# Wait lists, weight loads in pieces and a new operation order in a two-layer recurrent-memory transformer kernel

## The chip, the cores and the metric

The kernel runs on one core of one Trainium2 chip. The metric is the device time of one execution in microseconds (us). Each kernel was executed several times, and the medians are quoted. A ratio is the mean time of one kernel's fast runs over that of the kernel before in the same rounds, so it is not quite the ratio of the medians that stand beside it. Engines: PE is TensorE, PEld its weight loads, DVE VectorE, ACT ScalarE, POOL GpSimd, SP the engine that issues most transfers. In the profile's lines L128, L131 or L138 is one helper that issues all matmuls; its line number differs from kernel to kernel.

## The reference

A segment-recurrent attention layer (A) and a gated feed-forward layer (B), both applied twice with the same weights. In A, each of 64 segments of 32 tokens attends to itself and to 8 memory tokens, and the output rows of the memory are the memory of the next segment. That makes the chain which everything else has to fit around.

```python
def _A_ref(x, mem0, Wq, Wk, Wv, Wo, seg_len):          # cut
    mem = mem0
    for s in range(n_seg):
        h = jnp.concatenate([mem, x[:, s*seg_len:(s+1)*seg_len, :]], axis=1)
        q, k, v = (jnp.einsum('btd,dhe->bhte', h, W) for W in (Wq, Wk, Wv))
        scores = jnp.where(mask, jnp.einsum('bhqe,bhke->bhqk', q, k) * scale, -1e9)
        o = jnp.einsum('bhqk,bhke->bhqe', _softmax(scores), v)
        o = jnp.einsum('bhte,hed->btd', o, Wo)
        mem = o[:, :M, :]
        outs.append(o[:, M:, :])
def _B_ref(x, W_gate, W_up, W_down):                    # cut
    return (relu(x @ W_gate) * (x @ W_up)) @ W_down
x = x + _A_ref(_layernorm(x), ...);  x = x + _B_ref(_layernorm(x), ...)
x = x + _A_ref(_layernorm(x), ...);  x = x + _B_ref(_layernorm(x), ...)
```

## The kernel before

The kernel first multiplies the weights together (Wq with Wk, Wv with Wo), then runs 68 steps in which the first application of A works on one segment and the second on the segment four behind. Four steps repeat as one **period**. In a step the memory's chain is: s_mem (scores, softmax on DVE and ACT), p_t (transpose), u_mem, un_mem (the new memory in PSUM), hi (ACT) and lo (DVE: memory minus hi), then selm on PE (it moves hi and lo to where the next step needs them). All other work (t_block, u_seg, un, the glu of layer B: names of groups of matmuls in the code) is filler beside that chain.

Python lists all operations, a small scheduler puts them in an order from two tables (SLOT, BIAS), and then semaphores are laid. What matters here is how an operation gets its waits:

```python
def _need(self, eng, reads, writes):
    need = {}                       # semaphore -> value, one per engine or transfer
    ...                             # writers of what is read, readers of what is overwritten
    out = []
    for src, val in need.items():
        if self.known[eng].get(src, 0) < val:       # this engine hasn't waited for it yet
            self.known[eng][src] = val
            out.append((self.sems[src].sem, val))
    return out
...
    for s, v in waits:
        E.wait_ge(s, v)
    fn(E).then_inc(ev.sem, 1)
```

In the built program one wait of this list, the first, stays on the instruction itself (**attached**); the others go to instructions of their own ahead of it, with one or two waits each (**stand-alone**; counts of stand-alone waits below are counts of these instructions). And how the feed-forward weights are loaded, as soon as the buffers that they reuse are free:

```python
for h, W, d, n in ((0, S.Wg, S.Wg_d, "Wg"), (1, S.Wu, S.Wu_d, "Wu")):
    S.q.add("dma", ..., E.dma_start(W, d[0:384, :]...), (), where[n] + [(n,)])              # 1344 KB
    S.q.add("dma", ..., E.dma_start(S.W3[64*h:64*h+64, :], d[384:448, :]), ...)             # 224 KB
S.q.add("dma", ..., E.dma_start(S.Wd, S.Wd_d...), (), where["Wd"] + [("Wd",)])              # 1568 KB
```

## Time and profile before

| | kernel before |
|---|---|
| median | 1586.51 us (1584.45 to 1588.66, 4 runs) |
| profiled span | 1582.5 us |
| pure stream of PE | 1461.6 us |
| lost by PE up to its last matmul's start | 116.9 us |
| mean period (13 periods) | 89.82 us |
| half clock | six stretches, 27.1 us together |

**Pure stream** and **lost time** are used all through this document. The stream is every matmul of the built program times the distance at which matmuls of its form follow one another in the records when nothing holds them, plus 96 ns per change of the array's tile shape. The start of a matmul in the records, less the stream up to it, is what PE has lost so far: by standing, by waiting or by half clock. It is an estimate worked out from records.

One more view, the list of waits of PE from 200 to 1480 us (whom it waited for: us in total, number of times, longest):

```profile
PE b L128 <- DVE lo L1061: 7.9, 11, 1.5
PE b L128 <- ACT TTs L773: 5.1, 10, 0.5
PE b L128 <- issue: 4.5, 10, 0.8
PE b L128 <- DMA PTs<-Ps: 3.2, 5, 0.8
PE b L128 <- DVE Em L958: 2.8, 12, 0.2
```

The names to the right of the arrow are what PE waited for: lo; TTs, the copy by which ACT empties a bank of PSUM for t_block; PTs, the transposed probabilities of the segment, which a transfer brings; Em, a step of the memory's softmax; "issue" is time with no wait that the profile shows. Read it as a ranking, not as a sum: a pipelined matmul row hides short gaps, so this list sees less than the start-to-start count. The longest item is lo, the end of the memory's chain.

### The profile page before, as it was taken

Reading aid. Unit: us, or ns where it says so; the run is one execution under the profiler, and the core shown is the slowest. Engines: PE = TensorE matmul, PEld = TensorE weight load, DVE = VectorE, ACT = ScalarE, POOL = GpSimd, SP = SyncE. Lnnn points to the kernel's source line nnn. Section 1 sums busy time; section 2 is a strip of 40 time slices with the busy share of each in tenths; the row PEclk is TensorE's granted clock in tenths of the full one; section 3 lists DMA queues with packets and bytes.
Section 4 is the critical chain, followed back from the end, with each engine's and each line's share of the span. In section 5 each row is a group of like instructions: output and inputs, shape, how many; then the busy total and the mean of one; then the engine's idle time right before and its main releaser. Section 6 shows DMA issues by size and latency. Waiting matters only on the chain. (4 is left out here: it accounts for less than half of the span.)

```text
span 1582.5 us, 82606 instructions
## 1 busy us (share of the span) xinstructions
PE 1509.5 (95%) x37849; PEld 1110.3 (70%) x37849; DVE 877.3 (55%) x2316; ACT 865.7 (55%) x2636; POOL 111.3 (7%) x259
## 2 busy tenths in 40 slices
PE   5979999999999999999999999999999999999998
PEld 2556666777676776777676777777677777767675
DVE  7434556555555656554554655555564655555554
ACT  5734554655555565655556565555556465554432
POOL 4000000000000000000000000000000000000000
PEclk9989999999999999999999999999999999999999
DMA  9920000101000101001000101000010001000000
GB/s 211 239 71 12 19 18 19 20 15 17 19 16 15 25 15 19 16 16 19 16 19 15 21 18 15 17 19 16 18 21 15 20 19 15 15 18 15 18 19 14
DMA packets 128715, 46.05 MB, mean 29 GB/s; under 512 B 117480, under 2 KB 127472, under 8 KB 128368
## 3 DMA queue, kind: packets, MB, share of 16 engines
q1 hardware_dynamic: 128016, 40.52, 12.5%
q8 instruction: 298, 4.88, 1.3%
q14 instruction: 49, 0.40, 0.1%
q10 hardware_dynamic: 352, 0.24, 0.1%
HBM read 10.33 MB, written 1.84 MB: 8 GB/s over the span
## 5 line engine op out<-in xcount | busy, mean ns | idle before, releaser
L128 PE MATMUL b<-hT,Mw 128*128 128x80 bf16 (+1 forms) x11424 | 442.0, 200 | 6.4 <-issue 5.2
L128 PEld LDWEIGHTS b<-hT,Mw 128*128 128x128 bf16 x11424 | 418.7, 100 | 24.7 <-issue 13.0
L773 ACT ACTIVATE TTs<-b 128x320 bf16<-128x320 f32 (+4 forms) x694 | 290.0, 420 | 5.4 <-PE b L128 4.2
L128 PE MATMUL b<-Nw,big 128*32 128x448 bf16 (+1 forms) x3504 | 291.2, 353 | 0.3 <-issue 0.3
L773 ACT ACTIVATE TTm<-b 128x80 bf16<-128x80 f32 (+5 forms) x696 | 161.6, 232 | 218.9 <-PE b L128 211.1
L128 PEld LDWEIGHTS b<-Nw,big 128*32 128x32 bf16 (+1 forms) x3504 | 139.7, 97 | 99.4 <-issue 3.2
L128 PE MATMUL b<-xBT,big 128*128 128x128 bf16 (+3 forms) x4900 | 206.8, 215 | 1.9 <-issue 1.1
L128 PEld LDWEIGHTS b<-xBT,big 128*128 128x128 bf16 (+1 forms) x4900 | 186.3, 102 | 17.0 <-issue 7.5
L128 PE MATMUL b<-Nw,UTm 128*32 128x448 bf16 x3752 | 191.7, 356 | 1.8 <-ACT UTm L773 1.3
L128 PE MATMUL b<-hT,M 64*64 64x80 bf16 (+2 forms) x7208 | 149.2, 199 | 13.8 <-ACT TTs L773 5.1
L128 PEld LDWEIGHTS b<-Nw,UTm 128*32 128x32 bf16 x3752 | 100.4, 97 | 82.3 <-issue 11.3
L128 PEld LDWEIGHTS b<-hT,M 64*64 64x64 bf16 (+1 forms) x7208 | 113.3, 108 | 46.5 <-issue 24.5
L773 ACT ACTIVATE big<-b 128x512 bf16<-128x512 f32 (+1 forms) x244 | 123.5, 551 | 38.8 <-PE b L128 37.5
L774 POOL COPY hK<-xn 32x448 bf16<-32x448 bf16 x136 | 75.0, 552 | 662.1 <-DVE xn L816 655.7
L774 DVE CAST TTm<-b 64x64 bf16<-64x64 f32 (+5 forms) x188 | 41.3, 219 | 142.0 <-PE b L128 140.1
L774 DVE CAST big<-b 128x512 bf16<-128x512 f32 x144 | 82.3, 597 | 67.0 <-PE b L128 66.8
L1227 ACT ACTIVATE gT<-b 128x512 bf16<-128x512 f32 (+2 forms) x128 | 69.4, 542 | 64.2 <-PE b L128 63.5
L773 ACT ACTIVATE UTm<-b 128x512 bf16<-128x512 f32 (+1 forms) x143 | 81.7, 574 | 38.2 <-PE b L128 38.2
L128 PE MATMUL b<-big,hB 128*128 128x448 bf16 (+1 forms) x574 | 99.8, 354 | 0.3 <-DVE hB L1228 0.3
L1228 DVE TENSOR_TENSOR hB<-gT,b 128x512 bf16<-128x512 bf16 (+2 forms) x128 | 77.8, 619 | 27.5 <-ACT gT L1227 14.8
L128 PE MATMUL b<-PTs,hK 40*64 40x512 bf16 (+1 forms) x1024 | 83.3, 364 | 9.7 <-DMA PTs<-Ps 5.6
L957 DVE TENSOR_REDUCE stat<-b 128x2 f32<-128x80 f32 (+1 forms) x67 | 15.9, 237 | 136.1 <-PE b L128 135.0
(112 smaller groups left out, 1600.1 us busy)
## 6 DMA issues: line engine op xcount, KB each, us to landing
big<-in_A_Wo_dram SPq DMA_DIRECT2D x3, 896.0 KB, 5.8
out_dram<-ys SPq DMA_DIRECT2D x32, 56.0 KB, 1.9
big<-in_B_W_down_dram SPq DMA_DIRECT2D x1, 1568.0 KB, 8.5
XA<-in_A_x_dram SPq DMA_DIRECT2D x28, 56.0 KB, 2.6
big<-in_B_W_up_dram SPq DMA_DIRECT2D x1, 1344.0 KB, 8.5
big<-in_B_W_gate_dram SPq DMA_DIRECT2D x1, 1344.0 KB, 11.5
PTs<-Ps SPq DMA_TRANSPOSE x67, 2.5
Nw<-in_A_Wo_dram SPq DMA_DIRECT2D x1, 896.0 KB, 6.5
```

Of the source, the lines that this page charges most:

```text
L128: ins = E.matmul(out, lhsT=lhsT, rhs=rhs, **kw)
L773: return E.activation(out(), src(), ACT.Copy)
L774: return E.tensor_copy(out(), src())
L957: S.dve(lambda E: E.tensor_reduce(st[:, 32:32 + nl], src(), AX.X, ALU.max), n, C.res(), [("sm", 0)])
L1227: S.act(lambda E, g=g, R=R, n=n: E.activation(S.gT[:, g, 0:n], R[0].b()[:, 0:n], ACT.Relu), n, R[0].res(), [("gT", g)])
L1228: S.dve(lambda E, g=g, R=R, n=n, fcs=fcs: E.tensor_tensor(S.hB[:, fcs[0]:fcs[-1] + 1, 0:w], S.gT[:, g, 0:n].rearrange("p (a b) -> p a b", ...
```

## The change

Its intent: fewer and better placed waits; weight loads that don't stand in front of the small transposes which the chain needs; and a new search of the order with a cost model that knows that an ACT or DVE instruction whose start partitions change is held until the one before has ended. The core of the diff (the tables of some 170 searched numbers, BIAS and SLOT, are replaced as a whole):

```diff
+        need = {src: val for src, val in need.items() if kn.get(src, 0) < val}
+        past = {src: self.seen[src, val] for src, val in need.items()}
         out = []
+        for src, val in sorted(need.items(), key=lambda x: -self.when[x]):
+            if not any(p.get(src, 0) >= val for other, p in past.items() if other != src):
+                out.append((self.sems[src].sem, val))
         for src, val in need.items():
-            if kn.get(src, 0) < val:
-                kn[src] = val
-                out.append((self.sems[src].sem, val))
+            for a, v in [(src, val)] + list(past[src].items()):
+                if kn.get(a, 0) < v:
+                    kn[a] = v
 ...
-        return 35.0 if b != "pe" else 140.0 if a == "act" else 95.0
+        return 60.0 if b == "pe" else 35.0
 ...
+        fit = {"act": 104.0, "dve": 84.0}
+        def start(e, o):
+            if e not in fit:
+                return free[e]
+            return max(0.0, free[e] + (-fit[e] if o.base == base[e] else 28.0))
 ...
+        def piece(n, i, out, src):
+            S.pieces.append(lambda key: S.q.add("dma", ..., E.dma_start(out, src), [key], where[n] + [(n, i)]))
+        for n, W, d, m in (("Wu", ..., range(4)), ("W3", ..., range(2)), ("Wg", ..., range(6)), ("Wu", ..., range(4, 6))):
+            ...                                    # 224 KB each
+        for i in range(7):
+            piece("Wd", i, S.Wd[:, 2 * i:2 * i + 2, :], ...)
 ...
     def mm(self, fn, cost, rd, wr, mode=0, alt=None):
+        due = bool(self.pieces) and q.cat in self.PACE.get(q.t, ())     # steps 0 and 1 only
+        key = [("pace", len(self.pieces))] if due else []
-        self.q.add("pe", ("pe",), {"pe": cost}, fn, rd, wr, mode=mode, alt=alt)
+        q.add("pe", ("pe",), {"pe": cost}, fn, rd, list(wr) + key, mode=mode, alt=alt)
+        if due:
+            self.pieces.pop(0)(key[0])             # this piece may go when that PE operation is done
```

`when` is the time at which the scheduler's model has an event end; `seen` is what the engine that set it had itself waited for, so that a wait implied by another one is recognised.

## The prediction

> **What bounds the kernel now.** I read the page first (busy shares and slices), then the sums by window, then the timeline around single gaps, and last the trace's records of starts and semaphore increments. The page:
>
> ```profile
> PE 1509.5 (95%) x37849; PEld 1110.3 (70%) x37849; DVE 877.3 (55%) x2316; ACT 865.7 (55%) x2636; POOL 111.3 (7%) x259
> ...
> PE   5979999999999999999999999999999999999998
> ...
> PEclk9989999999999999999999999999999999999999
> DMA  9920000101000101001000101000010001000000
> ```
>
> TensorE (PE) is nearly full from the third slice on (each slice is 40 us), both copy engines stand at 55%, and the DMA engines matter in the first two or three slices only. So the end is set by PE: the time of its stream plus its gaps. Four steps of the recurrence repeat as one period. Two of them in the sums by window (busy us and instruction counts, then granted clock, DMA share, GB/s):
>
> ```profile
> 245.67:335.86 90.19, 88.07 (x2223) 65.88 (x2219) 50.26 (x127) 50.80 (x154) 5.79 (x14) 1.00 0.09 18
> 335.86:426.11 90.25, 88.03 (x2222) 65.87 (x2219) 50.27 (x127) 51.09 (x154) 5.79 (x14) 1.00 0.10 18
> ```
>
> Only 2.15 us of 90.2 shows as idle, but a busy matmul row is pipelined. I therefore took the start-to-start distance of neighbouring matmuls from the records (36 ns for 128x80, 189.5 for 128x448, 56 for 128x128, and so on) and called everything above that, plus 96 ns where the tile shape of the array changes, a gap. This gives 3.02 us of gaps per period, 45 us in 200 to 1480 us, and 97 us in the whole run, the slow-clock stretches of the start included. The largest kind in the period, from the timeline (start, length, engine, line, operation):
>
> ```profile
> 783.60 1.69 PE L128 MATMUL b<-Nw,big 128*32 128x448 bf16 x32
> 783.82 0.54 ACT L1060 ACTIVATE hi<-b 128x448 bf16<-128x448 f32 x1 [1.64 <-PE b L128]
> 784.47 0.63 DVE L1061 TENSOR_TENSOR lo<-b,hi 128x448 bf16<-128x448 f32 x1 [1.00 <-ACT hi L1060]
> ...
> 785.21 0.13 PEld L128 LDWEIGHTS b<-selm,hi 128*32 128x32 bf16 x4 [0.37 <-issue]
> ```
>
> The new memory leaves PE as hi and lo, and the next PE operation (selm) needs both. PE does 32 other matmuls meanwhile, then stands. The records show that lo's semaphore came 135 ns before selm's first matmul.
>
> The start has another cause:
>
> ```profile
> 73.76 0.37 SPq L731 DMA_DIRECT2D big<-in_B_W_down_dram  x1
> 74.22 0.65 SPq L727 DMA_DIRECT2D big<-in_B_W_gate_dram  x1
> 76.23 2.04 SPq L866 DMA_TRANSPOSE PTs<-Ps  x1
> ...
> 86.36 0.64 PE L128 MATMUL b<-PTs,hK 40*64 40x512 bf16 x2 [2.40 <-DMA PTs<-Ps]
> ```
>
> The small transpose PTs was issued at 76.2 and landed at 86.1 us, against 2.5 us in the page's list of issues: 2.9 MB of down and gate weights were in front of it (12 us at the 241 GB/s of slice two). PE stood 2.4 us, and its clock was halved:
>
> ```profile
> 82.90:93.10 10.20, 7.65 (x197) 6.32 (x193) 4.22 (x18) 2.93 (x11) 0.00 (x0) 0.50 0.43 79
> ```
>
> **What the Trainium skill says.** (1) Perfetto Trace Analysis, Identifying Dependency Chains: an instruction that waits for several engines may get EventSemaphore instructions ahead of it. The trace agrees: 606 on PE (51 ns each), 369 on DVE (21 ns), 116 on ACT (17 ns). In the built program the first wait in the list stays on the instruction and the others become such instructions. (2) TensorE: Matmul & The Clock Gate, Part 1: after an idle window of some 3.4 us the array runs at half rate. The trace agrees: seven pieces at 0.5, of 3.4 or 10.2 us. (3) TensorEngine Tiling (Array Packing), Key Properties: a change of tiling mode drains the array. Here the step from a 128x80 full matmul to a 64x64 tile takes 132 ns and not 36. (4) VectorE: DVE Perf Modes, Two Vector instructions with no wait between them: an instruction whose start quadrant differs from the one before is held. The trace agrees, for ACT too: with no wait between, the next starts 104 ns before the end of the one before if quadrants agree (ACT), 24 ns after it if not; on DVE 84 before, 31 after.
>
> **Part 1, the waits.** Where the last event to arrive sits on the instruction, PE's first matmul follows 43 ns later; where it sits on a stand-alone wait, 135 ns later. The same pair is 23 and 93 ns on DVE, 23 and 83 on ACT. So "latest first" is worth 92 ns where PE really waits. The trace has 143 such boundaries, 8 a period; 143 x 92 = 13 us at most, if every one of them stayed. Standalone waits fall from 605 to 367 on PE, from 369 to 108 on DVE and from 198 to 11 on SP; one that was satisfied long ago costs PE nothing (with one ahead, 128x40 matmuls still follow at 25 ns), so that count itself is worth about 0.
>
> **Part 2, the new order.** Counting matmuls of the built programs with the same distances, PE's pure stream is 1461.6 us before and 1463.9 after: 774 tile changes become 796, all of the added ones in the first and last steps, and the repeated period is equal at 86.2 us. So nothing is gained in the stream; gains are in gaps alone. I counted, in the built order, how much PE work lies between a producer and its consumer in one period, and held it against the latency that the trace shows:
> - un_mem to selm (hi, lo): 1824 ns before. Of it 92 (PE) and 70 (DVE, lo waits for hi by a stand-alone wait) go: 1662. Work between: 1695, 2074, 1624, 1036 ns before; 1695, 4727, 1624, 3420 after. Gap 0.89 us a period before, 0.04 after. **This is the main gain: 0.85 x 14.2 periods = 12 us.**
> - u_mem to un_mem: 925 ns with the wait attached; least work between 976 before, 597 after: 0.07 becomes 0.33.
> - s_mem: least work 686 before, 415 after, against some 510: adds 0.1.
> - t_block and u_seg, which wait until ACT has emptied a bank: 0.78 + 0.37 before. 3 x 92 ns go. Quadrant changes fall from 560 to 425 on ACT and 562 to 518 on DVE, so ACT's queue is 135 x 128 ns = 17 us shorter, and some of its lateness should go. I take 0.65 after.
> - PTs late (0.27), gaps inside runs of matmuls with no wait at all, which I take for instruction fetch (0.47), small ones (0.17): unchanged.
> After: 0.04 + 0.33 + 0.1 + 0.65 + 0.27 + 0.47 + 0.17 = 2.03 us. Saved 1.0 us x 14.2 = **14 us**.
>
> **Part 3, the pieces.** Weights come as 21 pieces of some 229 KB, and only one stands ahead of the first PTs, so the 2.4 us stall and most of the 10.2 us at half clock (up to 5 us) should go. Against that, the first two steps now run with little PE work beside their chain: taking the waits that step two of the kernel before shows (1.29 for p_t, 0.45 for u_mem, 0.70 for un_mem, and some 1.0 for m_t and t_block), I get about 4 us for each of two steps, and one or two halved windows of 3.4 us. From 68 to 139 us the kernel before loses 20.5 us to its stream; after I expect 14, less 2.3 for the added tile changes and a microsecond for weights that are awaited earlier. Net **3 to 4 us**.
>
> **The end** (1480 us on) has 12.5 us of gaps, among them hi/lo waits with 1139 and 1506 ns between and after now 1695 and 1726: **2 us**.
>
> Sum: 14 + 4 + 2 = 20 us, so 1566; rounded for what a longer search may have found that my counting does not see, **1564 us**, 1.4% faster.
>
> **The rivals.**
> A. *PE's stream is the bound and gaps only move.* For it: equal stream, and new tight places (597, 415 ns). Then the 92 ns alone remain and part is lost again: 1575 to 1584.
> B. *The search removed nearly all waits.* It now has delays that fit the trace (104 and 84 ns of overlap, 24 to 31 when held). All waits on ACT and DVE are 2.1 us a period, 30 us, with start and end 40: 1546. Against: the tight places above are visible in the order.
> C. *The pieces become a wait.* Each piece waits on SP until the one before it in its group has landed, and later PTs transposes stand behind them in SP's order. If a piece takes 3 us, the last lands at about 121 us, some 6 us before down needs it. Should it be late, PE stands 3 to 6 us and the clock halves: 1568 to 1575.
> D. *A new order upsets ACT or DVE queues* (55% busy, bunched): slower by some us a period; 1590. Little speaks for it.
>
> **Range and chances.** A ends at 1580, B at 1548; the two bracket the sum, so 1549 to 1579. Faster by over 2% means under 1554.4 us, which needs most of B: 0.2. Slower by 2% needs 1618: 0.01. Within: 0.79.
>
> **What would show it.** Right: a period of 89.2 us instead of 90.2; no gap ahead of selm over 0.1 us; PE's first matmul 43 ns after the last event almost everywhere; PTs landing within 5 us at the start and no 10 us stretch at half clock; the gap ahead of un_mem grown to 0.3 us once a period. Wrong: selm still late, which would mean that hi or lo start late in their queues; a period below 88.5 us (B); the first 140 us no shorter (C), with PE waiting for a weight piece.

## The result

The changed kernel is correct and takes **1565.52 us** (median; 1564.91 to 1567.49, 4 runs) against 1586.51 in the same rounds: ratio 0.987, 95% interval 0.9853 to 0.9887. So it is 1.3% faster, a microsecond and a half from the predicted time. The page's lines of busy shares and slices:

```profile
PE 1505.9 (96%) x37969; PEld 1106.3 (71%) x37969; DVE 868.0 (56%) x2353; ACT 858.3 (55%) x2599; POOL 112.0 (7%) x259
...
PE   5889999999999999999999999999999999999997
...
PEclk9989999999999999999999999999999999999998
```

They look like those of before: the third slice still has a dip of the clock, and the last slice now has one too. The two periods that answer to those in the prediction:

```profile
242.30:330.26 87.96, 87.34 (x2225) 65.67 (x2224) 49.73 (x130) 50.33 (x151) 5.79 (x14) 1.00 0.10 18
330.26:418.26 88.00, 87.38 (x2226) 65.68 (x2225) 49.63 (x130) 50.32 (x152) 5.80 (x14) 1.00 0.08 18
```

They are 2.2 us shorter, where the prediction had 1.0. Over 13 periods the mean is 88.33 us (before 89.82). The waits of PE from 200 to 1480 us:

```profile
PE b L138 <- ACT big L798: 5.3, 15, 0.4
PE b L138 <- DVE UTm L799: 3.6, 14, 0.3
PE b L138 <- issue: 2.6, 5, 1.1
PE b L138 <- DVE lo L1097: 0.5, 1, 0.5
```

lo has fallen from 7.9 us to 0.5, and the waits for TTs, PTs and Em have left the list. New are two places that come once a period: u_seg waits for ACT to empty a bank (big), un_mem for u_mem's copy (UTm). One selm of it, from the timeline (start, length):

```profile
774.15 1.69 PE L138 MATMUL b<-Nw,big 128*32 128x448 bf16 x32
774.38 0.54 ACT L1096 ACTIVATE hi<-b 128x448 bf16<-128x448 f32 x1 [2.42 <-PE b L138]
774.95 0.63 DVE L1097 TENSOR_TENSOR lo<-b,hi 128x448 bf16<-128x448 f32 x1 [1.71 <-ACT hi L1096]
775.66 0.18 PE L138 MATMUL b<-selm,hi 128*32 128x16 bf16 x4
```

lo now starts 0.03 us after hi ends (before 0.11), and selm 0.08 us after lo ends (before 0.14, rounded as the rows are). PE's 32 other matmuls take until selm; there is no gap left.

So the period gained more than predicted. Where did it go? The lost time by stage says it (us; one profiled execution each; "first" is the start of the first matmul; the last column is stream plus lost time, the start of the last matmul). The rows below the second are the experiments, and the profiled executions of the two kernels differ by 18.6 of the medians' 21.0 us, since that of before (1584.34 us) was one of its faster ones:

| kernel | first | to 80 | 80 to 160 | 160 to 1480 | 1480 on | stream | last matmul |
|---|---|---|---|---|---|---|---|
| before | 6.3 | 18.7 | 19.8 | 58.5 | 13.6 | 1461.6 | 1578.5 |
| **after** | 8.3 | 21.1 | 17.6 | 36.1 | 12.8 | 1463.9 | 1559.9 |
| new waits, old order (e1) | 6.3 | 17.9 | 17.1 | 48.2 | 9.5 | 1461.6 | 1560.5 |
| drop only (e5) | 6.0 | 17.6 | 17.1 | 52.7 | 9.5 | 1461.6 | 1564.6 |
| latest first only (e6) | 6.2 | 19.4 | 17.5 | 48.5 | 10.3 | 1461.6 | 1563.5 |
| new waits and pieces, old order (e7) | 6.3 | 17.3 | 14.5 | 46.8 | 11.3 | 1461.6 | 1557.9 |
| old waits, new order and pieces (e2) | 8.6 | 23.2 | 21.1 | 50.4 | 16.1 | 1463.9 | 1583.3 |
| after, big loads, badly placed (e4) | 8.4 | 24.7 | 26.9 | 34.9 | 12.1 | 1463.9 | 1570.9 |
| after, big loads (e4b) | 8.6 | 20.8 | 18.6 | 37.7 | 11.9 | 1463.9 | 1561.5 |
| after, xAT later (e3) | 8.5 | 18.9 | 16.3 | 36.0 | 11.3 | 1463.9 | 1554.9 |
| old head of 553, then after (e8a) | 6.6 | 16.8 | 13.3 | 36.3 | 11.9 | 1464.2 | 1549.1 |
| old head of 998, then after (e8b) | 5.8 | 17.9 | 16.2 | 37.5 | 12.3 | 1464.0 | 1553.7 |

From 160 to 1480 us the changed kernel gains 22.4 us. Up to 160 us it loses 2.2 (44.8 before, 47.0 after), and its stream is 2.3 us longer, all of that in the first and last steps; the end gains 0.8. The first 160 us were expected to bring 4 us with the longer stream already taken off, so 8.5 us went the other way there and in the stream together.

One cause is visible in SP's queue. After (start, length of the issue):

```profile
8.57 4.04 SPq L622 DMA_TRANSPOSE Nw<-in_A_Wq_dram  x1
18.06 1.19 SPq L902 DMA_TRANSPOSE xAT<-xn  x1
19.29 3.88 SPq L622 DMA_TRANSPOSE Nw<-in_A_Wk_dram  x1
...
39.66 3.76 SPq L622 DMA_TRANSPOSE big<-in_A_Wv_dram  x1
```

Before:

```profile
8.58 3.95 SPq L605 DMA_TRANSPOSE Nw<-in_A_Wq_dram  x1
12.57 3.81 SPq L605 DMA_TRANSPOSE Nw<-in_A_Wk_dram  x1
...
33.60 1.19 SPq L866 DMA_TRANSPOSE xAT<-xn  x1
34.83 4.42 SPq L605 DMA_TRANSPOSE big<-in_A_Wv_dram  x1
```

The new order puts the transpose of the second segment's input, xAT, fourth. It can't go before POOL has copied the first segment out of the same buffer, so SP stands from 12.6 to 18.1 us, and every weight behind it comes 5 us late. PE's first un_mem starts at 81.87 us instead of 74.38.

The clock is a second suspect. This profile of after has 34.3 us at half clock, that of before 27.1. The stretch that the pieces were to remove is still there, and a longer one stands near the end. The columns are the window, its length, busy us of PE, PEld, DVE, ACT and POOL, then the granted clock:

```profile
94.60:104.80 10.20, 7.87 (x122) 4.49 (x122) 3.54 (x18) 1.86 (x7) 0.00 (x0) 0.50 0.42 124
1531.70:1535.10 3.40, 2.23 (x54) 1.37 (x50) 2.33 (x8) 2.48 (x10) 0.00 (x0) 1.00 0.52 43
1535.10:1545.30 10.20, 9.64 (x140) 5.75 (x144) 2.23 (x5) 2.39 (x4) 0.00 (x0) 0.50 0.01 2
```

But one profile is a poor witness of the clock. The record has the granted clock of every run, and twice its distance from 1, times the span, is the run's time at half clock: 22.7 us on average for before (29 runs, 9.5 to 31.8) and 27.1 for after (9 runs, 15.6 to 34.5). In e1's four runs 15.7 us more at half clock went with 3.1 us more time, so by that estimate the 4.4 us between the averages are worth about one microsecond. And the second profile of the changed kernel (run after_again below) has 17.1 us at half clock up to 160 us, no more than before, and still loses 46.7 us there. So the clock is not what made the start worse. Near the end there is a pattern: the eight profiles with the new order have one stretch of 6.8 to 13.7 us there, the five with the old order have none over 3.4.

### The profile page after: what moved, and what is told of

Read it like the earlier page. It is cut to its first block, busy times and chain, and to the rows that moved or that the text cites. A ratio compares the mean times of both kernels' runs of the same rounds, so it can differ in the third digit from the quotient of the medians.

```text
span 1563.9 us, 81992 instructions
## 1 busy us (share of the span) xinstructions
PE 1505.9 (96%) x37969; PEld 1106.3 (71%) x37969; DVE 868.0 (56%) x2353; ACT 858.3 (55%) x2599; POOL 112.0 (7%) x259
## 4 chain that ended last, share of the span: by engine, by line
PE 92%; DVE 3%; SPq 2%; ACT 2%; issue 1%; DMA 1%; POOL 0%; POOLq 0%; DVEq 0%
PE b L138 92%; SPq L622 2%; ACT hi L1096 1%; ACT big L798 1%; DVE UTm L799 1%; DMA Nw<-in_A_Wo_dram 0%; DVE selm L658 0%; DMA PTs<-Ps 0%; DVE seln L661 0%; DVE stat L845 0%; DVE part L1192 0%; DVE lo L1097 0%; ACT UTm L798 0%; DVE big L799 0%; DVE xn L852 0%
## 5 line engine op out<-in xcount | busy, mean ns | idle before, releaser
L138 PE MATMUL b<-hT,Mw 128*128 128x80 bf16 (+1 forms) x11424 | 436.7, 200 | 9.2 <-issue 8.6
L138 PEld LDWEIGHTS b<-hT,Mw 128*128 128x128 bf16 x11424 | 415.3, 100 | 22.7 <-issue 14.3
L138 PE MATMUL b<-Nw,big 128*32 128x448 bf16 (+1 forms) x3540 | 295.1, 356 | 1.8 <-DVE big L799 0.8
L798 ACT ACTIVATE TTs<-b 128x320 bf16<-128x320 f32 (+5 forms) x658 | 278.4, 426 | 3.7 <-PE b L138 3.7
L798 ACT ACTIVATE TTm<-b 128x80 bf16<-128x80 f32 (+5 forms) x658 | 153.2, 235 | 137.7 <-PE b L138 131.9
L798 ACT ACTIVATE big<-b 128x512 bf16<-128x512 f32 (+1 forms) x258 | 128.5, 560 | 35.2 <-PE b L138 35.0
L799 DVE CAST TTm<-b 64x64 bf16<-64x64 f32 (+4 forms) x226 | 48.6, 216 | 176.3 <-PE b L138 174.7
L138 PE MATMUL b<-hT,M 64*64 64x80 bf16 (+2 forms) x7208 | 142.8, 198 | 2.0 <-DVE M L799 1.2
L798 ACT ACTIVATE hT<-b 64x16 bf16<-64x16 f32 (+1 forms) x134 | 24.0, 179 | 125.9 <-DVE hT L799 88.0
L799 DVE CAST TTs<-b 64x256 bf16<-64x256 f32 (+4 forms) x226 | 90.5, 401 | 2.7 <-PE b L138 2.6
L1096 ACT ACTIVATE hi<-b 128x448 bf16<-128x448 f32 x67 | 36.5, 544 | 91.6 <-PE b L138 91.6
```

The costliest lines, as they stand in the source:

```text
L138: ins = E.matmul(out, lhsT=lhsT, rhs=rhs, **kw)
L798: return E.activation(out(), src(), ACT.Copy)
L799: return E.tensor_copy(out(), src())
L1096: S.act(lambda E: E.activation(S.hi[:, :], C.b()[:, 0:D], ACT.Copy), D, C.res(), [("hi",)])
```

## The experiments

Eleven kernels ran in three calls; all were correct. The kernels of one call share the runs of the kernel before. The first four had 1586.27 us (11 runs), the second four 1586.79 (9 runs), the last three 1589.10 (9 runs). The three calls ran on three chips. Because of that last figure, kernels of different calls are compared by ratio, and the interval of a single ratio is already some 2 to 4 us wide to either side: a difference of 2 us between two calls is a hint and no proof.

My theory after the result: the wait rule and the order each bring about half of the gain in the period, the pieces a few us at the start, and the order takes a part back at the start and end. Rivals: all of the period's gain is the waits' alone; or the order's alone; or the start is bound by something else.

### e1: the new waits in the old order

```diff
 # before.py, with after.py's _need and _mark; order, slots and loads untouched
+        for src, val in sorted(need.items(), key=lambda x: -self.when[x]):
+            if not any(p.get(src, 0) >= val for other, p in past.items() if other != src):
+                out.append((self.sems[src].sem, val))
```

> The kernel before with the changed kernel's wait rule alone (implied waits dropped, latest first); order, slots and weight loads stay. My theory (the prediction's part 1): PE really waits at 8 boundaries a period, and each becomes 92 ns shorter, with 70 ns more for the un_mem to selm pairs because lo no longer waits by a stand-alone wait: 0.8 to 1.0 us a period, 11 to 14 us in 14 periods, a few more at start and end: 1570 to 1575 us, period about 89.0, PE's first matmul 43 ns after the last event nearly everywhere; the gap ahead of selm stays once or more a period (0.4 us or so), because the order gives it too little work. Rival A (gaps only move to the next wait): 1580 to 1586. Rival S (the saving in the steady state, 24 us, is the waits' alone, order adds nothing): 1562 to 1566.

Measured: **1567.93 us** (1566.35 to 1569.49), ratio 0.9888 (0.987 to 0.9907). The wait rule alone brings 18.3 of the 21 us; that is 2 us better than I had expected and 2 us short of rival S. The period is 89.11 us as expected, and 10.3 us of the gain lie between 160 and 1480 us; another 3.5 come before 160 us and 4.1 at the end, which I had put at "a few". The last two are not to be read finely: the profiled execution is the fastest of e1's four and has the least half clock (14.0 us; by the granted clocks the four average 21.1, and before 22.7). PE's waits from 200 to 1480 us:

```profile
PE b L138 <- ACT TTs L784: 6.2, 14, 0.5
PE b L138 <- DVE lo L1072: 4.6, 8, 0.6
PE b L138 <- DMA PTs<-Ps: 4.0, 6, 1.0
```

lo falls from 7.9 to 4.6 us, while TTs (the bank that ACT empties for t_block) rises from 5.1 to 6.2. So it is not 92 ns at each of eight places. Counted start to start, the gap ahead of selm falls from 948 to 396 ns a period; at three waits a period that is 184 ns each, close to the 92 of PE and 70 of DVE. Of the t_block waits (849 to 897 ns) nothing is saved: PE only comes there earlier and stands for the same ACT. Rival A holds for that part, my theory for the chain. Not all of the period's gain can be laid to waits, though: 348 of the 822 ns that e1 saves (table under e2) are gaps inside runs of matmuls, where nothing is waited for, and why those fell is not shown.

### e5 and e6: each half of the wait rule

```diff
 # e5, drop only                                   # e6, latest first only
-  for src, val in sorted(need.items(), ...):      +  for src, val in sorted(need.items(), ...):
+  for src, val in need.items():                   +      out.append((self.sems[src].sem, val))
       if not any(p.get(src, 0) >= val ...):       -      if not any(p.get(src, 0) >= val ...):
           out.append(...)                         -          out.append(...)
```

> The kernel before with one half of the wait rule: implied waits are dropped, but the rest stay in the order of before. Stand-alone waits on PE fall from 606 to 421, as with the full rule. In the trace of before, PE's last event sat on a stand-alone wait at 167 places; in this program 69 of them have it on the instruction, with the full rule 158. Theory (only the place of the last event counts, 92 ns each): 69/158 of the full rule's 18 us, 8 us, to 1576 to 1580. Rival (the number of stand-alone waits counts, whatever the order): 1567 to 1570, as with the full rule.

> The kernel before with the other half: nothing is dropped (606, 369 and 116 stand-alone waits on PE, DVE and ACT, as before), but the event that the scheduler has as the latest is put first and so sits on the instruction. Theory (place alone): all 158 places of the full rule change, 1567 to 1570, within 2 us of it. Rival (number): the time of before, 1583 to 1586. Between them, some 1573 to 1577, if on DVE and ACT, which are not the bound but feed it, the number costs 20 ns each on the way to what PE waits for.

Measured: drop only **1571.00 us**, ratio 0.9906 (0.9892 to 0.9919); latest first only **1573.20 us** (1568.80 to 1575.44), ratio 0.9909 (0.9894 to 0.9924). Each half alone brings some 14 us, so they are not additive: they mostly reach the same waits by two ways. My 8 us for e5 was wrong because places are not equal. Its selm gap is 370 ns a period, as small as e1's: dropping one implied wait puts the right one on the instruction there, on PE and on DVE. At t_block and u_seg, where its last event still comes on a stand-alone wait, the gaps stay (899 and 395 ns), and the stage from 160 to 1480 us has 52.7 us of loss against e1's 48.2.

e6 keeps all 606 stand-alone waits of PE and loses 48.5 us in that stage, against 48.2 in e1 with 421. So in the steady state the number of stand-alone waits costs nothing that these two profiles can tell, and the place of the last event is what counts. Over the whole run e6 is 3 us behind e1 (by the ratios, whose intervals overlap), in the range that I had set for a number that counts on DVE and ACT; its profile has 10.2 us of half clock at 79.9 where e1 has 3.4 at 84.9. Whether the number caused that, or the phase of the clock's windows, stays open.

### e2: the old waits in the new order

```diff
 # after.py, with before.py's _need and _mark
-        for src, val in sorted(need.items(), key=lambda x: -self.when[x]):
-            if not any(...):
+        for src, val in need.items():
+            if kn.get(src, 0) < val:
+                kn[src] = val
```

> The changed kernel with the wait rule of before; order, slots and pieces stay. My theory: the new order gives un_mem to selm so much other work (1624 ns at least) that 1824 ns of latency is late again by some 0.2 to 0.3 us in three of four steps, and the boundaries where PE still waits (u_seg, un_mem, s_mem) pay 92 ns more each: 0.8 us a period, 10 to 13 us over the changed kernel: 1575 to 1579. If waits and order simply add, e1's saving and this one's sum to the whole 21 us. Rival O (order alone brought the steady gain): 1566 to 1569. Rival W (waits alone): 1584 or more.

Measured: **1584.90 us** (1579.08 to 1589.16), ratio 0.9992 (0.9973 to 1.001): the order and the pieces without the new waits bring nothing. The time is that of rival W, but not for its reason. From 160 to 1480 us e2 gains 8.1 us on before (58.5 to 50.4; period 89.23), and gives it all back: 2.3 us ahead of the first matmul, 4.5 to 80 us, 1.3 to 160 us, 2.5 at the end, 2.3 of stream. It has 48.4 us of half clock, but the profiled execution is the slowest of its six (they average 34.3 by the granted clocks), so some 4 us of these losses are that execution's own. PE's waits from 200 to 1480 us:

```profile
PE b L131 <- ACT big L791: 5.2, 15, 0.4
PE b L131 <- issue: 5.2, 16, 0.6
PE b L131 <- DVE UTm L792: 4.8, 14, 0.3
PE b L131 <- DVE lo L1090: 0.6, 1, 0.6
```

These are the two new places of the changed kernel, and TTs is gone with the old waits too. The gaps by kind (ns per period, start to start, 14.2 periods):

| waits for | before | e1 | e2 | after | predicted after |
|---|---|---|---|---|---|
| selm (hi, lo) | 948 | 396 | 360 | 73 | 40 |
| t_block (ACT, DVE empty a bank) | 849 | 897 | 32 | 27 | 650 with u_seg |
| u_seg (the same) | 407 | 333 | 544 | 568 | (above) |
| un_mem | 79 | 8 | 430 | 338 | 330 |
| s_mem | 0 | 0 | 200 | 118 | 100 |
| u_seg, PTs not landed | 252 | 326 | 15 | 35 | 270 |
| inside runs, no wait | 554 | 206 | 718 | 307 | 470 |
| all | 3200 | 2378 | 2511 | 1569 | 2030 |

In the period the two halves nearly add: 0.82 us for the waits and 0.69 for the order make 1.51 of the 1.63 together. At selm alone they don't: each of them saves 0.55 to 0.59 us there without the other, and both together 0.88.

### e7: the pieces in the old order

```diff
 # e1, plus after.py's pieces and PACE; PE's order is unchanged, matmul by matmul
-        for h, W, d, n in ((0, S.Wg, S.Wg_d, "Wg"), (1, S.Wu, S.Wu_d, "Wu")): ...   # five big loads
+        for n, W, d, m in (...): ... piece(n, i, ...)                              # 21 pieces
```

> The kernel before with the full new wait rule and the 21 pieces; PE's order is that of before, matmul by matmul. The prediction's part 3 in the order that it was worked out from: the 2.4 us wait for the first PTs and the half clock behind it go, 3 to 5 us less than with the wait rule alone (1567.9): 1563 to 1565. Rival C (pieces are awaited by PE at the glu): 1568 to 1572. Rival N (hidden anyway): 1567 to 1568.

Measured: **1566.07 us** (1563.69 to 1566.74), ratio 0.9873 (0.9858 to 0.9888). By the ratios that is 2.4 us less than e1, where I expected 3 to 5. It comes where it should: 17.1 to 14.5 us of loss between 80 and 160 us. PE waits for no transfer between 60 and 160 us, and its half clock there falls from 10.2 to 6.8 us. Over all runs, e7 averages 13.3 us at half clock and e1 21.1. Rival C has no support. That the time is below e1's is likely and not certain: the intervals of the two ratios overlap.

With the same waits and the pieces, old and new order now stand side by side: 0.9873 for e7, and 0.987 and 0.9849 for the changed kernel. **The new order as a whole brings 0 to 4 us, and the runs do not tell more.** In the table it wins 10.7 us from 160 to 1480 us, and it loses 2.0 ahead of the first matmul, 3.8 to 80 us, 3.1 to 160 us, 1.5 at the end and 2.3 in the stream.

### e4 and e4b: the big loads in the new order

```diff
 # after the scheduler has run on after.py: the 21 pieces are taken out of the order, five big loads put in
+        big("Wu", ...); big("Wd", ...); big("Wg", ...); big("W3", ...) x2
 # e4: each as early as its buffers allow;  e4b: up behind the last Wo, the W3 pair behind the first PTs, as in before
```

> The changed kernel with the gate, up and down weights in the five large loads of before, each issued as soon as the buffers are free; the order on PE, ACT, DVE and POOL is unchanged, instruction by instruction. The prediction's part 3: the first PTs stands behind some 3 MB again, PE stands 2 to 6 us at the first u_seg and its clock is halved: 1568 to 1572, 3 to 6 us slower than the changed kernel. Rival: the first two steps are bound by the recurrence's own chain and by the half clock (which the changed kernel still has, 10.2 us at 94.6 to 104.8), and what stands ahead of PTs is hidden: 1565 to 1567.

> The earlier run with five big loads in the changed kernel's order put the up load ahead of the last Wo load, which PE needs first, and two small loads ahead of the first PTs, so it charged the pieces with faults of my placing (PE waited 3.4 us for Wo and 8.4 us behind down). Here the five stand as in the kernel before: up behind the last Wo, gate and down ahead of the first PTs, the two small ones behind it. Theory (part 3): 3 to 6 us over the changed kernel, 1568.5 to 1571.5, with the first PTs landing some 10 us after its issue. Rival: as much as the 11 us of the earlier run, 1575 to 1577, which would mean that this order has less other work to put beside a late PTs.

e4 gave **1576.50 us**, ratio 0.9935 (0.9921 to 0.9949), 11 us over the changed kernel, but the experiment was faulty. As early as possible was earlier than in the kernel before, and PE's list of waits from 60 to 140 us shows what that did:

```profile
PE b L138 <- DMA big<-in_B_W_down_dram: 8.4, 1, 8.4
PE b L138 <- DMA big<-in_A_Wo_dram: 3.4, 1, 3.4
```

e4b gave **1568.20 us** (1565.07 to 1569.89), ratio 0.9883 (0.9869 to 0.9896). By the ratios that is 2.1 us over the changed kernel of the first call and 5.4 over that of the third. PE waits 2.9 us for the first PTs; in the two profiles of the changed kernel it is 0 and 1.2 us. So the wait that the pieces shorten is shown, and the runs put their worth at some 2 to 5 us in either order; they don't tell it closer, and they don't tell the wait's part from the half clock's.

### e3: one transfer moved

```diff
 # after the scheduler has run on after.py: xAT of the second segment goes behind the last Wk load,
 # and the three copies that read it behind the first Wo load; PE and ACT unchanged
+        self.q.order = od[:i] + [... not moved, to Wk3] + [x] + [... not moved, to Wo0] + [moved] + od[k + 1:]
```

> The changed kernel with one transfer moved: the transposition xAT<-xn of the second segment, which stands fourth in SP's queue and makes all later weight transpositions wait 5.4 us, is issued behind the last Wk load, and the three copies that read it move behind it on DVE and POOL; PE's and ACT's order are unchanged. My theory: the first Wv transposition is issued at some 35 us and not 39.7, PE's first un_mem starts 4 to 6 us earlier than 81.9, and all later follows: 1559 to 1562 us, 3 to 6 us faster than the changed kernel. Rival 1: the weights were not what PE waited for at the start (the layer norms or the products of the weights were): 1565, unchanged. Rival 2: the earlier start is lost again to half-clock stretches at 80 to 105 us: 1563 to 1566.

Measured: **1560.68 us** (1558.80 to 1563.92), ratio 0.9842 (0.9824 to 0.9859). By the ratios that is 4.4 us under the changed kernel of the first call, and 1.1 under that of the third. SP's queue no longer stands:

```profile
33.55 1.19 SPq L913 DMA_TRANSPOSE xAT<-xn  x1
34.79 3.68 SPq L633 DMA_TRANSPOSE big<-in_A_Wv_dram  x1
```

un_mem starts at 77.24 us, 4.6 earlier, as the theory had it. Rival 1 doesn't hold; how much of the earlier start is kept to the end (rival 2) the runs leave between 1 and 4 us.

### e8a and e8b: the old head, the new period

```diff
 # after.py; HEAD holds the first 553 (998) operations of e7 with their engines
+HEAD = ("52g 8a 17d 0s 10a 11a 9a 12a 16d 13a 14g 15g 19d ...")
         self.q.run()
+        head = [...]                                   # HEAD, decoded
+        q.replay(head + [(o, o.fixed, o.mode) for o in q.order if o not in first])
         q.emit()
```

`replay` takes the operations in the given order and hands out the PSUM banks anew, the one that was freed first going first.

> The first 553 operations of the earlier run with before's order, new waits and pieces (all engines, through the scores of the second memory step), then everything else in the changed kernel's order, with the banks handed out anew. Counting lost time as the start of PE's last matmul less its pure stream: the changed kernel lost 8.3 us ahead of its first matmul, 21.1 to 80 us and 17.6 from 80 to 160; the earlier run 6.3, 17.3 and 14.5. Theory (the changed kernel's new head gives back what its period gains): 5.8 us less to 80 us and about a microsecond fewer tile changes, with the period unchanged at 88.3: 1558 to 1560. Rival (the two heads differ only in when work is done, and the join costs as much): 1563 to 1566.

> The same with the first 998 operations, through the sixth memory step at some 180 us. Theory: 8.9 us less to 160 us than the changed kernel and up to 2 us fewer tile changes, less 1 to 2 us for the join, where work already done leaves PE short: 1555 to 1558. Rival: 1563 to 1566. In both the loss from 160 to 1480 us should stay near 36 us; near 47 would say that the gain of the new order needs its own head.

> The changed kernel once more, unchanged, beside the two joined orders on the same chip and in the same rounds: 1565 to 1567, as before. If it differs by more than 2 us, the comparisons of kernels from different calls need that much more room.

Measured in the same rounds: e8a **1554.93 us** (1552.77 to 1555.80, ratio 0.9784, 0.976 to 0.9808), e8b **1556.44 us** (1555.20 to 1559.57, ratio 0.9798), the changed kernel again **1565.20 us** (1561.44 to 1568.45, ratio 0.9849, 0.9825 to 0.9873). e8a is 10.3 us faster than the changed kernel, and 2.2% faster than the kernel before. Its page:

```profile
PE 1501.4 (97%) x37999; PEld 1105.7 (71%) x37999; DVE 867.5 (56%) x2348; ACT 859.5 (55%) x2604; POOL 112.0 (7%) x259
...
PEclk9999999999999999999999999999999999999998
```

The third slice of the clock is full now, but the changed kernel's page of the same call has the same line, so that is no mark of the old head. The half clock up to 160 us is 6.8 us (17.1 in the changed kernel of the same call); over all runs it is 18.0 us for e8a and 25.0 for the changed kernel. Against the changed kernel of the same call (8.6, 21.3, 16.8, 35.9 and 12.8 us by stage) it loses 10 us less up to 160 us and the same in the period, whose mean is 88.32 us: the new period doesn't need its own head. That shows that the head of the new order, and not the pieces or the waits, took back what the period had gained. I had expected 1558 to 1560: between 80 and 160 us e8a beats e7 as well (13.3 against 14.5). Its stream is not shorter (1464.2), so the tile changes were not where it gained, as I had thought they would be in part.

## Why the prediction was right or wrong

The time was right to 1.5 us, but the sum was not right term by term: 14 + 4 + 2 was predicted, and the profiled runs show 22.4 from 160 to 1480 us, -2.2 up to there, -2.3 in the stream and +0.8 at the end. So 8.4 us too little on one side and 9.7 too much on the other cancelled, and two more microseconds had been added to the sum without a count: that the time is so near is luck.

- **The bound and the method.** Right. PE's stream is the bound, equal in the period, and all of the gain is in gaps.
- **Part 1, the waits.** The mechanism is right. PE follows an attached event after 43 to 46 ns nearly everywhere now (between 160 and 1480 us 86 of 88 late places are attached; 29 of 171 before). The mis-sized term is "13 us at most": alone the rule measured 18.3 us. The count of PE's own places left out DVE's 70 ns and, above all, the first 160 us and the end, where it brought 7.6 us (in e1's fastest execution). On the other side, not every place pays: t_block's gap did not shrink in e1. "The count itself is worth about 0" holds in the steady state (e6), and is open for the rest.
- **Part 2, the order.** The size of the main gain, selm, is right: 0.85 us of a period was predicted, 0.88 measured (948 to 73 ns). Its owner is not: 0.55 of it comes with the new waits in the old order (e1), and over the whole run the new order adds 0 to 4 us to the new waits and pieces (e7), where 12 were booked on it. The prediction's own counts would even give 1.12 us for before (129 + 200 + 788 ns), not 0.89. The new gaps, 0.33 for un_mem and 0.1 for s_mem, came as counted, and t_block with u_seg came at 0.60 for 0.65, though otherwise distributed: t_block's went entirely, u_seg's grew. The step that failed is "PTs late (0.27), gaps inside runs of matmuls (0.47) ... unchanged": they fell to 0.04 and 0.31. The first is the new order's doing (e2 has it, e1 has not). And 3.02 us of gaps for before was too little for all 14.2 periods, which have 3.20, as 97 us was for the whole run: start to start it is 110.6 (116.9 less the 6.3 ahead of the first matmul). So 1.63 us a period and not 1.0.
- **Part 3, the pieces, "net 3 to 4 us".** This is the step that failed most. The pieces shorten the wait for PTs as was said, and are worth 2 to 5 us (e7, e4b). But I reckoned the start of the changed kernel from 68 us on, and never looked at the order ahead of that. There SP's queue stood for xAT (e3: 1 to 4 us), and the rest of the head cost more than that (e8a: 10.3 us together). The 10.2 us at half clock did not go; they stand at 94.6 us in the first profile of after, and 6.8 at 97.5 in the second. Nor did the wait for PTs start them in the kernel before: PE stood from 84.0 to 86.4 us, and the clock had fallen at 82.9, behind a window in which PE was busy 2.07 of 3.40 us:

```profile
79.50:82.90 3.40, 2.07 (x112) 1.97 (x113) 0.43 (x2) 1.09 (x5) 0.18 (x1) 1.00 1.04 411
```

Whether the wait made the stretch longer is open. A sentence of the prediction, that the trace agrees with the half clock after an *idle* window, in seven pieces, is cut for this reason; there are six, and this one has no idle window ahead of it.

- **The end, 2 us.** 0.8: two gaps of 0.8 us with no wait and then a wait of 1.73 us for the last Ps came together, and 10.2 us at half clock began there (6.8 in the second profile). The kernel before has 3.4 us at a time in its end.
- **The rivals.** B (1546) named a period under 88.5 us as its sign, and the period is 88.33; B was right on the period and wrong on the start. A describes e1's t_block, and no more (the range took its far end as 1580, where A itself says 1584). C and D are refuted: no wait for a weight piece, no longer queue.

Still open: what causes the gaps inside runs. In the profile of before, 19 of the 21 such gaps over 150 ns end 1.0 to 1.6 us after a 16 KB packet of the queue that the page calls "q8 instruction" has ended. Such packets come every 5.1 us in the middle, so some 2 or 3 of 21 would fall so by chance. A stricter count, of gaps between equal matmuls alone, gives 132 of 136 over all thirteen profiles. The gaps without a wait right ahead of the two long half-clock stretches of after (1.49 us at 93.9 us, 0.82 and 0.84 near the end) end 1.5 to 1.6 us after such a packet too. This fits a wait for instructions, and no run tested it. The sum of these gaps differs from 0.2 to 0.7 us a period between kernels, without a reason that I can show; the two kernels with the old wait rule (before and e2) have the most.

## What to carry to other kernels

Put the event that comes last on the instruction itself, above all on the chain that everything waits for; dropping implied waits does the same where it lets that event move up, and in the repeated period the number of stand-alone waits hardly matters. A search on a model pays where the model is true, here in the repeated period. Its gains must be checked stage by stage, since this model knows neither the half clock nor a queue that stands behind its head, and the search lost at the start what it won in the period. Lost time by stage, the matmul's start less its pure stream, shows that at once, and then the better head and the better period can be joined. One profile shows one execution, though: what the clock did is read from the granted clock of all runs.

## What the Trainium skill lacked or had wrong

- Perfetto Trace Analysis, Identifying Dependency Chains, tells that stand-alone waits are inserted, and gives no cost. Here PE follows an attached event after 43 ns and one on a stand-alone wait after 135 ns, DVE after 23 and 93, ACT after 23 and 83. One satisfied long ago costs PE nothing measurable in the repeated period (48.5 against 48.2 us of loss with 606 and 421 of them on PE).
- TensorE: Matmul & The Clock Gate, Part 1, has the half clock after an idle window, and the full clock after one busy window of 3.4 us. Here it fell after a window in which PE was busy 2.23 of 3.40 us, and it stayed at half for 10.2 us while PE was busy 9.64 of them. So less than idle is enough to lose it, and one busy window is not always enough to get it back.
- TensorEngine Tiling (Array Packing), Key Properties, says that a change of the tiling mode drains the array; the cost, some 96 ns each here, is missing.
- VectorE: DVE Perf Modes, Two Vector instructions with no wait between them, gives the rule of the held instruction for Vector alone. ACT shows the same: 104 ns of overlap where the start quadrants agree, 24 ns of pause where they don't. In the trace of before, all 163 instructions of ACT that the rule holds (with no wait ahead of them) start after the end of the one before, and all 764 others ahead of it; on DVE it is 82 and 303.
- Runtime: NRT & Kernel Launch, Instruction fetch mechanics, has the 16 KiB blocks in which instructions come and calls the cost of crossing into one mostly hidden. It lacks the gaps inside runs of matmuls that follow such packets here (19 of 21 within 1.0 to 1.6 us after one has ended; up to 0.7 us a period); that the packets cause them is not shown.
